# Three edits to a scheduled attention kernel: later loads, a values-stationary first layer, and another choice of the tiles whose exp runs on VectorE

## Chip, cores and metric

The kernel runs on one core of one Trainium2 chip. The metric is the device time of one execution in microseconds (us). A quoted time is the median of the runs of one kernel. All runs told of here are fast runs: none is over 1.5% above the fastest of the same kernel. A ratio is the mean time of one kernel's fast runs over the mean time of the kernel before in the same rounds on the same chip, so it is not quite the ratio of the medians quoted beside it. Intervals are 95%.

## The reference

Four layers act on 2048 tokens of width 512, with 32 heads of 16. Each is a layer norm, an attention, an output projection and a residual. Layers 0 and 2 are "memory attention", layers 1 and 3 full attention.

```python
# layers 0 and 2: four segments of 512 tokens
for s in range(4):
    p = softmax(qs @ ks.T / 4 + causal_mask)
    a_mem = phi(qs) @ M / (phi(qs) @ z + 1e-6)       # read-out of the memory
    outs.append(g * a_mem + (1 - g) * (p @ vs))      # g = sigmoid(beta), per head
    M = M + phi(ks).T @ vs;  z = z + sum(phi(ks))    # memory chain: s needs s-1
# layers 1 and 3: all 2048 keys
p = softmax(q @ k.T / 4);  o = p @ v
# every layer: x = x + attention(layernorm(x)) @ wo
```

A *block* (L, s) below is layer L with the queries of tokens 512·s to 512·s+511.

## The kernel before

A list scheduler, written in Python, runs while the kernel is built. It keeps an estimated clock for each engine and lays down one fixed, in-order program for TensorE (PE), ScalarE (ACT), VectorE (DVE), GpSimd (POOL) and the DMA queue.

The main loop goes: three score tiles (128×512 each) by PE into PSUM, one exp over all three by ScalarE into a ring of 18 buffers, then the products with V (PV) by PE. Projections, layer norms, memory work and evictions run as background threads between the groups.

```python
def emit_group(self, tiles, mode):             # scores -> exp, cut
    sc.add("pe", ... matmul(out, lhsT, rhs) ...)          # S, four row groups
    self.dx_scores(tiles, mode)                            # maybe one tile for VectorE
    sc.add("act", ... activation(dst, src, ACT.Exp, scale=SCALE) ...)   # 128x1536
    # masks on POOL for the diagonal blocks of layers 0 and 2
```

Some tiles leave ScalarE. A *dx group* is four score tiles whose exp is computed by VectorE: four evictions `dz` and seven arithmetic steps on 2048 columns. The rule that picks them before looks at the unit in work and asks for ten groups' worth of its tiles still unscored:

```python
def dx_pick(self):
    ...
    for u in seen:                              # the unit in work, and the next
        if u["kind"] != "B" or u["pvn"] < 12 or u["no"] < self.dx_no: continue
        rest = [tl for tl in u["tiles"] if not tl.get("dx") and "slot" not in tl]
        if len(rest) < 4 * (DX_LEFT + 1): continue         # DX_LEFT = 9
        four = rest[-4:]
def dx_scores(self, tiles, mode):
    if mode != "w" or len(tiles) < 3: return   # not in blocks with background work ("m")
def g_dx(self, four):                          # a thread; each yield lets others in
    o = dv(... tensor_scalar(F, lo, ...)); yield W(o)      # dF
    o = dv(... tensor_scalar(E, hi, ...)); yield W(o)      # dE
    ...                                                    # dP1 dP2 dP3 dP4
    o = dv(... tensor_tensor(E, E, Pz, ALU.add))           # dE2
```

In layers 0 and 2 the exp tile is stationary and V (17 columns per head: 16 and a one, for the sum) streams. The result is token-major, so a DMA transpose must turn it for the output projection, and its buffer `tokk` is the one that the memory chain uses for phi(k):

```python
def norm_A(self, u, par, bank, alloc):          # cut
    if s > 0: self.ensure(("nd", L, s))         # the memory read-out must be done
    dv(... reciprocal(r1, acc[:, :, 16]) ...)   # 128x16
    dv(... tensor_tensor(r2, r2, om, ALU.mult) ...)     # times 1-g
    dv(... tensor_tensor(dst, acc4, rb, ALU.mult) ...)  # into ot; adds a_mem if s > 0
    if self.cnt[key] == 8:
        zs = self.take_oT(L, s)
        if self.tok_mem is not None: self.ensure(("dM",) + self.tok_mem)
        for i in range(4): o = self.dma_T(self.tokk[...], self.ot[:, i, :], ...)
        self.set_ev(("otfree", L, s))
def t_mem(self, L, s, prio):                    # phi(k).T V, cut
        if self.oT_hold[0] is not None: yield ("ev", [("op",) + self.oT_hold[0]])
        for c in range(NCH): o = self.dma_T(self.tokk[...], self.kA[:, u, c, :], ...)
def t_nd(self, L, s, prio):                     # read-out phi(q) M into ot
        yield ("ev", [("M", L, s), ("otfree", L, s - 1)] + [("q", L, s, c) for c in range(NCH)])
# pv_ready: the last PV step of either half of a unit waits for ("nd", L, s)
```

All loads are issued at the start, ahead of the first transposes on the same queue:

```python
ld_x(0); ld_w(0, "A_wq"); ld_w(1, "A_wk"); ld_w(2, "A_wv")
for s in range(1, 4): ld_x(s)
# then beta, woA, wB (1.5 MB), woB
def g_ln(self, L, s):                           # cut
    for i, t in enumerate(t4):
        xn = self.xn[:, i % 2, :]               # two buffers
        o = sc.add("dve", ... tensor_scalar(xn, xt, mu, r1, ...))
        o = self.dma_T(self.xT[...], xn, ...)
```

The softmax here doesn't subtract the row's maximum and nothing guards it: scores larger than these inputs give would overflow.

## Time and profile before

The median of the first three runs is 2208.72 us (2208.08 to 2210.48). The profiled span is 2208.9 us.

The first line is that of the page of the kernel before for engine totals: busy time, share of the span, number of instructions.

```profile
PE 1735.5 (79%) x13064; PEld 458.4 (21%) x13138; DVE 1551.6 (70%) x2436; ACT 2011.4 (91%) x1594; POOL 263.4 (12%) x562
```

ScalarE, at 91%, looks like the limit, but the share is an average. The next lines are the table by stretch of the kernel before: start:end, length, then the busy time of each engine with its instruction count, the granted PE clock, the DMA share and GB/s.

```profile
0.00:75.00 75.00, 34.28 (x258) 12.45 (x262) 36.40 (x93) 25.90 (x31) 21.99 (x49) 0.86 0.45 120
75.00:370.00 295.00, 243.00 (x2396) 96.31 (x2418) 174.76 (x431) 235.22 (x224) 96.89 (x239) 0.76 0.10 19
370.00:500.00 130.00, 102.39 (x612) 18.57 (x609) 61.05 (x89) 129.46 (x104) 0.00 (x0) 0.52 0.00 1
500.00:1340.00 840.00, 662.92 (x5154) 184.04 (x5185) 642.01 (x983) 776.84 (x590) 116.96 (x206) 0.63 0.05 9
1340.00:1500.00 160.00, 132.71 (x1073) 41.02 (x1080) 55.11 (x130) 150.15 (x135) 27.60 (x69) 0.69 0.04 8
1500.00:2209.00 709.00, 560.23 (x3581) 106.02 (x3586) 582.30 (x716) 693.79 (x515) 0.00 (x0) 0.55 0.01 4
```

Read the fourth figure after the length, ACT. In the first two rows it is busy 25.9 + 235.2 of 370 us: 109 us are lost there. From 370 to 500 us it is full while VectorE works 61 of 130 us: there is room on VectorE for more of ScalarE's work. From 1500 us on ScalarE is saturated.

The start of the kernel before, in the timeline: start, length, engine, line, operation, names, shapes and count; in brackets the idle time before it and what ended it.

```profile
12.50 21.27 SPq L369 DMA_TRANSPOSE xT<-xn  x5
21.97 0.82 DVE L577 TENSOR_SCALAR xn<-x_tok,lnmv,lnr 128x512 bf16<-128x512 bf16 x2 [11.42 <-DMA xT<-xn]
26.27 3.57 PE L527 MATMUL ps<-xT,wA 128*128 128x512 bf16 x8 [23.83 <-DMA xT<-xn]
32.33 1.51 ACT L908 ACTIVATE pT<-ps 128x512 bf16<-128x512 f32 x2 [30.26 <-PE ps L902]
```

The third normalize waits 11.42 us for the buffer that the first transpose reads, the first projection starts at 26.27 us, and the first exp at 32.33 us. (The 21.27 us of the first line span five transposes and the pauses between them.)

Two groups of instructions of the kernel before matter later: columns as in the timeline without the times, then busy us, mean ns of one, and the idle time of the engine before them with its main releasers. The first is the exp (all shapes), the second the PV matmuls of layers 0 and 2.

```profile
L908 ACT ACTIVATE pT<-ps 128x1536 bf16<-128x1536 f32 (+1 forms) x1518 | 1977.7, 1463 | 159.3 <-PE ps L902 144.6 <-issue 3.5 <-PE ps L1018 3.1
L1112 PE MATMUL ps<-vA,pT 128*128 128x17 bf16 x2560 | 96.0, 175 | 16.3 <-POOL pT L931 7.6 <-DVE dz L1021 3.3 <-DVE q L542 1.8
```

Nearly all of ScalarE's idle time before an exp is ended by a score matmul: PE is late, for whatever reason. The 2560 narrow matmuls cost 96 us of PE time in both memory layers together; 43.9 us of it fall in layer 0.

### The profile page before, as it was taken

To read this page: it belongs to the slowest core of one execution; us is meant where nothing else is said; L and a number is where in the kernel's file an instruction comes from. 1 tells how busy PE (TensorE), PEld (TensorE's weight loads), DVE (VectorE), ACT (ScalarE), POOL (GpSimd) and SP (SyncE) were. 2 spreads that over 40 slices of the span, in tenths; PEclk is the share of its full clock that TensorE was granted. 3 is DMA by queue.
4 is the path that set the end of the run, shared out by engine and by line. 5 is a ranking of instruction groups with operands and counts; after the bars stand their busy time and mean duration, and the time that the engine had idled before them with its cause. 6 is when DMAs were issued, how large, how long until landed. Compare 5 with 4: busy or idle time off the path is not lost.

```text
span 2208.9 us, 32937 instructions
## 1 busy us (share of the span) xinstructions
PE 1735.5 (79%) x13064; PEld 458.4 (21%) x13138; DVE 1551.6 (70%) x2436; ACT 2011.4 (91%) x1594; POOL 263.4 (12%) x562
## 2 busy tenths in 40 slices
PE   3878887787778787777777888787778887787777
PEld 1333332111222112121122223221111111111111
DVE  4677534177888777887768766136778888888887
ACT  2778788998999979989989998999999999999998
POOL 2443230000023001220011201110000000000000
PEclk8778767556755775556856588566565555556555
DMA  5110100000000000000100000000000000000000
GB/s 143 30 30 11 20 11 20 0 1 13 8 1 1 20 18 2 1 10 11 20 1 1 11 11 11 1 20 1 1 10 1 1 10 1 1 1 11 1 1 10
DMA packets 73162, 26.25 MB, mean 12 GB/s; under 512 B 65840, under 2 KB 72496, under 8 KB 73008
## 3 DMA queue, kind: packets, MB, share of 16 engines
q1 hardware_dynamic: 73008, 24.14, 4.9%
q8 instruction: 103, 1.69, 0.3%
q14 instruction: 51, 0.42, 0.1%
HBM read 6.30 MB, written 2.10 MB: 4 GB/s over the span
## 4 chain that ended last, share of the span: by engine, by line
ACT 44%; PE 27%; issue 12%; DVE 11%; DMA 3%; POOL 2%; SPq 1%; ACTq 0%; DVEq 0%
ACT pT L908 43%; PE ps L527 10%; PE ps L902 9%; PE ps L1127 5%; DMA xT<-xn 2%; POOL pT L931 2%; PE ps L1112 2%; DVE dz L1021 1%; PE ps L1018 1%; DVE db L1063 1%; DVE dz L1061 1%; SPq L369 1%; DVE df L1046 1%; DVE lnst L559 1%; DMA tokk<-ot 1%
## 5 line engine op out<-in xcount | busy, mean ns | idle before, releaser
L908 ACT ACTIVATE pT<-ps 128x1536 bf16<-128x1536 f32 (+1 forms) x1518 | 1977.7, 1463 | 159.3 <-PE ps L902 144.6
L902 PE MATMUL ps<-q,kB 32*128 32x512 bf16 x3708 | 717.5, 554 | 289.5 <-ACT pT L908 283.3
L1127 PE MATMUL ps<-pT,vB 128*17 128x512 bf16 x3708 | 510.7, 547 | 12.5 <-DVE dz L1021 3.4
L1021 DVE TENSOR_SCALAR dz<-ps 128x512 int32<-128x512 f32 x388 | 267.3, 689 | 152.8 <-PE ps L1018 144.3
L931 POOL TENSOR_SCALAR_AFFINE_SELECT pT<-pT 128x256 bf16<-128x256 bf16 (+2 forms) x519 | 237.0, 486 | 721.0 <-ACT pT L908 719.6
L902 PEld LDWEIGHTS ps<-q,kB 32*128 32x128 bf16 x3708 | 132.6, 97 | 855.5 <-ACT pT L908 793.3
L1018 PE MATMUL ps<-q,kB 32*128 32x512 bf16 x388 | 227.1, 585 | 1.2 <-DVE dz L1021 1.1
L902 PE MATMUL ps<-q,kA 32*128 32x512 bf16 (+3 forms) x1024 | 134.5, 404 | 52.8 <-ACT pT L908 50.0
L1127 PEld LDWEIGHTS ps<-pT,vB 128*17 128x17 bf16 x3708 | 89.1, 90 | 375.6 <-issue 337.8
L1196 DVE STREAM_TRANSPOSE T<-ps 128x512 f32<-128x512 f32 x88 | 62.8, 713 | 130.0 <-PE ps L1127 128.5
L1046 DVE TENSOR_SCALAR df<-dz 128x2048 f16<-128x2048 uint16 x97 | 120.2, 1239 | 3.3
L1061 DVE TENSOR_TENSOR dz<-dz,df 128x2048 f16<-128x2048 f16 x97 | 119.6, 1233 | 2.7
L1057 DVE TENSOR_TENSOR dz<-dz,df 128x2048 f16<-128x2048 f16 x97 | 119.3, 1230 | 2.1
L1063 DVE TENSOR_TENSOR db<-db,dz 128x2048 int16<-128x2048 int16 x97 | 118.8, 1225 | 2.4
L1052 DVE TENSOR_SCALAR db<-dz 128x2048 int16<-128x2048 int16 x97 | 119.2, 1229 | 0.0
L1112 PE MATMUL ps<-vA,pT 128*128 128x17 bf16 x2560 | 96.0, 175 | 16.3 <-POOL pT L931 7.6
L527 PE MATMUL ps<-xT,wA 128*128 128x512 bf16 x239 | 74.2, 440 | 36.0 <-DMA xT<-xn 23.8
L1112 PEld LDWEIGHTS ps<-vA,pT 128*128 128x128 bf16 x2560 | 81.5, 102 | 76.2 <-POOL pT L931 51.2
L527 PE MATMUL ps<-xT,wB 128*128 128x512 bf16 x225 | 74.6, 459 | 14.4 <-DMA xT<-xn 6.9
L826 DVE TENSOR_TENSOR x_tok<-x_tok,ps 128x512 bf16<-128x512 bf16 x64 | 43.9, 687 | 57.1 <-PE ps L527 56.4
L577 DVE TENSOR_SCALAR xn<-x_tok,lnmv,lnr 128x512 bf16<-128x512 bf16 x64 | 25.9, 425 | 66.6 <-DMA xT<-xn 59.9
L1127 PE MATMUL ps<-db,vB 128*17 128x512 bf16 x388 | 56.6, 574 | 16.7 <-DVE db L1063 15.4
(79 smaller groups left out, 1071.3 us busy)
## 6 DMA issues: line engine op xcount, KB each, us to landing
x_tok<-in_A_x_dram SPq DMA_DIRECT2D x16, 128.0 KB, 4.5
out_dram<-x_tok SPq DMA_DIRECT2D x4, 512.0 KB, 2.9
wB<-in_B_wqkv_dram SPq DMA_DIRECT2D x1, 1536.0 KB, 8.4
xT<-xn SPq DMA_TRANSPOSE x64, 2.4
wA<-in_A_wq_dram SPq DMA_DIRECT2D x1, 512.0 KB, 4.3
wA<-in_A_wk_dram SPq DMA_DIRECT2D x1, 512.0 KB, 5.2
wA<-in_A_wv_dram SPq DMA_DIRECT2D x1, 512.0 KB, 6.4
woA<-in_A_wo_dram SPq DMA_DIRECT2D x1, 512.0 KB, 4.9
```

The costliest lines, as they stand in the source:

```text
L527: return self.sc.add("pe", lambda e: e.matmul(out, lhsT, rhs, start=start, stop=stop), reads=reads, bank_ops=[(bank, "w", alloc)], emit=la ...
L902: sc.add("pe", (lambda out, lhsT, rhs: lambda e: e.matmul(out, lhsT, rhs, start=True, stop=True))(out, lhsT, rhs), reads=reads, bank_ops=[ ...
L908: o = sc.add("act", lambda e: e.activation(dst, src, ACT.Exp, scale=float(SCALE)), writes=[self.b_pT[s0 + i] for i in range(n)], bank_ops= ...
L931: om = sc.add("pool", (lambda ap, pat: lambda e: e.affine_select(ap, ap, pattern=pat, compare_op=ALU.is_ge, fill=0.0, base=0, channel_mult ...
L1018: sc.add("pe", lambda e: e.matmul(out, lhsT, rhs, start=True, stop=True), reads=reads, bank_ops=[(bank, "w", alloc)], emit=True, name="SX" ...
L1021: o = sc.add("dve", lambda e: e.tensor_scalar(dst, out, float(EXP_C * 65536.0), -126.0 * 65536.0, op0=ALU.mult, op1=ALU.max), writes=[self ...
L1046: o = dv(lambda e: e.tensor_scalar(F, lo, 2.0 ** -16, -0.5, op0=ALU.mult, op1=ALU.add), bz, bF, "dF", 1.24)
L1057: o = dv(lambda e: e.tensor_tensor(Pz, Pz, F, ALU.mult), bF + bP, bP, "dP2", 1.24)
L1061: o = dv(lambda e: e.tensor_tensor(Pz, Pz, F, ALU.mult), bF + bP, bP, "dP4", 1.24)
L1063: o = dv(lambda e: e.tensor_tensor(E, E, Pz, ALU.add), bP + bE, bE, "dE2", 1.24)
L1112: sc.add("pe", (lambda o0, slot, p0, v, first: lambda e: e.matmul(self.ps[:, o0:o0 + 17], self.pT[:, slot, p0:p0 + 128], v, start=first, s ...
L1127: sc.add("pe", (lambda out, v, rhs, start, stop: lambda e: e.matmul(out, v, rhs, start=start, stop=stop, skip_group_check=True))(out, v, r ...
```

## The change

The intent has three parts.

**Loads.** Only the first segment and the three weights of layer 0 are loaded ahead. The rest is issued by a thread behind the transposes of each segment. The first segment's normalize uses four buffers.

**Layer 0 attention.** V becomes stationary, as in layers 1 and 3, and the exp tile streams. The result is normalized through 32×32 block transposes on VectorE, into its own buffers. The memory read-out is transposed by DMA into `m0` and added. The memory chain of layer 0 no longer shares a buffer with the output.

**VectorE exp.** The tiles of a dx group are picked by their distance: at least 56 tiles ahead, in any block from the end of layer 0 on. A group that will be needed soon goes ahead of other work on VectorE.

```diff
+DX_SLACK = 4.0
+DX_LEAD = 56
-DX_LEFT = 9
@@ setup
         ld_x(0)
+        ld_w(1, "A_wk")
         ld_w(0, "A_wq")
-        ld_w(1, "A_wk")
         ld_w(2, "A_wv")
-        for s in range(1, 4):
-            ld_x(s)
-        ... beta, woA, wB, woB at once
+        def rest():
+            yield ("ev", [("xT", 0, 0)])
+            ld_x(1)
+            ... beta, woA
+            yield ("ev", [("xT", 0, 1)])
+            ld_x(2)
+            ... wB in four chunks
+            yield ("ev", [("xT", 0, 2)])
+            ld_x(3)
+            ... woB
+        self.spawn(rest(), -1.0, "LD")
@@ g_ln
+            if L == 0 and s == 0 and i >= 2:
+                xn, bxn = self.ot[:, i, :], self.b_ot[i]
@@ t_nd
-            yield ("ev", [("M", L, s), ("otfree", L, s - 1)] + [("q", L, s, c) for c in range(NCH)])
+            yield ("ev", [("M", L, s)] + ([("otfree", L, s - 1)] if L > 0 else []) + [("q", L, s, c) for c in range(NCH)])
+            if L == 0:
+                yield ("ev", [("pvdone", L, s - 1)])
+                for i in range(4):
+                    self.dma_T(self.m0[:, :, i * 128:(i + 1) * 128], self.ot[:, i, :], ...)
@@ t_out
-            self.oT_hold[slot] = None
+            if L:
+                self.oT_hold[slot] = None
@@ unit_A: layer 0 with V stationary
+                    pv = [(None, par, j, 0, 512, 0, va(par, j, 0), vr(0))]
+                    ...
@@ norm, layer 0
+            dv(lambda e: e.scalar_tensor_tensor(on, T1[:, :, 0:16], om, rb, op0=ALU.mult, op1=ALU.mult), ...)
+                o = dv(lambda e: e.transpose(dst, onf), ...)
+                if s > 0:
+                    self.ensure(("nd", L, s))
+                    o = dv(lambda e: e.tensor_tensor(dst, dst, mem, ALU.add), ...)
@@ pv_ready
-        if last and u["kind"] == "A" and u["s"] > 0 and ("nd", ...) not in self.ev:
+        if last and u["kind"] == "A" and u["s"] > 0 and (u["L"] > 0 or u["pvd"] == 4) and ("nd", ...) not in self.ev:
@@ dx_pick
-            if len(rest) < 4 * (DX_LEFT + 1):
-                continue
+            n += far.get(id(u), len(rest))
+            if u["kind"] != "B" or u["no"] < self.dx_no or n < DX_LEAD or len(rest) < 8:
+                continue
@@ new
+    def dx_ahead(self, u, need):
+        ...                                   # n: tiles still to come before this group's PV
+        return DVE_AHEAD if 0.45 * n < need + DX_SLACK else DX_AHEAD
@@ dx_scores
-        if mode != "w" or len(tiles) < 3:
+        if ("op", 0, 3) not in self.ev or len(tiles) < 2:
             return
```

## The prediction

> **What bounds the kernel now.** The page shows ScalarE busy 91% of 2208.9 us; the chain that ended last puts 43% on the exp activation. The table by stretch splits this. From 1500 us to the end ScalarE is busy 693.8 of 709 us: saturated. From 370 to 500 us it is busy 129.5 of 130 while VectorE works only 61. From 500 to 1340 us: 777 of 840. In the first 370 us (layer 0 and the start of layer 1) only 261: 109 us are lost to latency, 31 of them before the first exp (32.3 us).
>
> **Startup.** All 6.3 MB of loads are issued by 12.5 us and the first four transposes come after them on the same queue. The first releases its buffer only at 21.97 us, while the median transpose takes 2.4 us. [...] The last of the four lands near 26.1. With only 1.5 MB of wA ahead, and four buffers, so that no normalize waits for a transpose, I expect it near 15: 10 to 12 us gained, all on the critical path.
>
> **Layer 0 attention.** 1280 matmuls of 17 columns (28 to 35 ns each) become 512 wide ones with V stationary, four side by side [...]. About 2560 columns a unit, at 0.55 us per four of 512, is 1.5 to 2.7 us against 2.2 to 2.8: an estimate, small gain. VectorE pays: a norm goes from 0.9 us (1.4 with memory) to transpose 0.71 + reciprocal 0.25 + scale 0.43, plus half of (0.71 + memory add about 0.4): some 20 us more over 32 norms. In return the output no longer shares the token-major buffer with phi(k), so the memory chain runs ahead, attention waits for it only before the last step of a unit, and output projection needs no DMA transposes. Of the 60 us of ScalarE idle between 75 and 370 us I expect 10 to 20 back. Evacuation copies on ScalarE rise by 22 (0.6 us each), which fills idle time and relieves VectorE by 15.
>
> **VectorE exp.** The built order has 107 groups instead of 97: 40 tiles leave ScalarE. In the saturated stretch ScalarE starts a group of three every 1.38 us, so a tile is worth about 0.45 us: 18 us at most. By unit: six more groups go to layer 1's first query block, nine to layer 3's first, five leave later blocks, where time is given back. VectorE pays 10.3 us a group, mostly where it idles. I expect 10 to 16 us net. PE waits on late VectorE groups (60 us in the list of waits) should shrink, but few of them reach ScalarE.
>
> **Sum.** 2208.7 - 11 - 4 (gates stall near 50 us) - 14 - 13 = about 2167 us (range 2142 to 2192). Chances: faster by over 2%: 0.45; within 2%: 0.52; slower: 0.03.
>
> **What would show it.** First exp near 20 to 22 us; ScalarE idle in the first 370 us falls from 109 to about 80; exp instructions 1501 instead of 1518; VectorE busy near 1660 us; the last stretch (layer 3, blocks 1 to 3) no shorter.
>
> **What would make it wrong.** Spread-out loads could delay later transposes of layer 0; the heavier VectorE norm could hold PSUM banks and stall PE; VectorE groups put first could delay evacuations, so that ScalarE idles more. On the good side, if the memory chain held layer 0, the gain there could be twice mine.

## The result

The changed kernel takes 2174.34 us (2173.01 to 2175.28, four runs) against 2209.6 us: ratio 0.984, interval 0.9823 to 0.9857. That is 35 us where 42 were predicted, inside the range and within 2%. A second measurement of the same kernel on another occasion (e9 below) gave 0.9837.

The totals of the changed kernel on its page:

```profile
PE 1706.2 (79%) x12290; PEld 426.3 (20%) x12370; DVE 1658.1 (76%) x2532; ACT 2004.1 (92%) x1599; POOL 274.9 (13%) x562
```

VectorE works 107 us more, as predicted (1660), ScalarE 7 us less. The table by stretch of the changed kernel, columns as before, without the last row:

```profile
0.00:75.00 75.00, 43.66 (x255) 13.88 (x260) 37.64 (x94) 40.34 (x47) 28.13 (x66) 0.82 0.46 118
75.00:370.00 295.00, 247.57 (x1786) 72.31 (x1806) 221.40 (x460) 261.28 (x256) 94.83 (x221) 0.78 0.09 17
370.00:500.00 130.00, 105.27 (x656) 19.46 (x654) 108.34 (x148) 127.84 (x98) 2.14 (x2) 0.54 0.02 5
500.00:1340.00 840.00, 652.93 (x5210) 185.01 (x5246) 633.24 (x979) 780.30 (x601) 116.99 (x206) 0.66 0.04 9
1340.00:1500.00 160.00, 125.38 (x1037) 36.61 (x1043) 122.56 (x210) 142.22 (x118) 32.84 (x69) 0.63 0.04 8
```

In the first 370 us ScalarE is now busy 40.3 + 261.3 us, so 68 us idle instead of 109: the gain is there. (At fixed times the two tables hold different work. Within layer 0 alone ScalarE was idle 97.6 of 327.0 us and is idle 59.5 of 296.8.) Look then at the last row: VectorE has gone from 55 to 123 us of work, as intended, yet ScalarE does not finish its own reduced work at the old pace. It was idle 9.9 us in this stretch and is now idle 17.8; over the whole of block (3,0) it is idle 10.4 of 275.1 us before and 21.4 of 270.1 now.

The start of the changed kernel in the timeline:

```profile
10.52 2.60 SPq L377 DMA_TRANSPOSE xT<-xn  x2
13.16 2.58 SPq L377 DMA_TRANSPOSE xT<-ot  x2
17.10 3.57 PE L553 MATMUL ps<-xT,wA 128*128 128x512 bf16 x8 [14.66 <-DMA xT<-ot]
19.62 0.69 DVE L585 BATCH_NORM_STATS2 lnst<-x_tok 128x6 f32<-128x512 bf16 x1 [8.16 <-DMA x_tok<-in_A_x_dram]
23.29 0.32 DVE L642 TENSOR_SCALAR q<-q,parm 128x512 bf16<-128x512 bf16 x1
24.16 0.60 ACT L960 ACTIVATE pT<-ps 128x512 bf16<-128x512 f32 x1 [1.72 <-PE ps L954]
```

The first projection starts 9.2 us earlier, the first exp 8.2 us earlier (24.16 against 32.33). The four transposes hold the queue for 5.2 us (10.52 to 15.74). Between projection and exp, VectorE first waits for the second segment's data, 8.16 us, and computes its statistics; the scaling of q that the first scores need stands behind that in VectorE's order.

The exp group of the changed kernel, and the PV matmuls of layer 0, which are now four widths of one line:

```profile
L960 ACT ACTIVATE pT<-ps 128x1536 bf16<-128x1536 f32 (+1 forms) x1501 | 1962.1, 1471 | 123.6 <-PE ps L954 92.4 <-PE ps L1086 14.4 <-issue 14.2
L1201 PE MATMUL ps<-pT,vA 128*17 128x512 bf16 x128 | 15.4, 457 | 7.2 <-POOL pT L983 3.4 <-DVE T L1273 2.3 <-DVE kA L568 1.3
L1201 PE MATMUL ps<-pT,vA 128*17 128x384 bf16 x128 | 13.8, 382 | 0.3 <-POOL pT L983 0.2
L1201 PE MATMUL ps<-pT,vA 128*17 128x256 bf16 x128 | 11.4, 321 | 0.1
L1201 PE MATMUL ps<-pT,vA 128*17 128x128 bf16 x128 | 8.7, 249 | 0.0
```

Two things to see. The idle time before exps fell from 159 to 124 us, but 14.4 us of it is now ended by L1086, the score matmul of a dx group, which hardly appeared before (3.1 us), and 14.2 us is "issue" (3.5 before). And the 512 wide matmuls of layer 0 sum to 49.3 us, but matmuls of different widths overlap: counted once, they keep PE busy 38.5 us. The narrow ones of layer 0 did so for 43.9 us, with 1240 of 1280 in the trace, and for 45.4 us in the trace of e1 below, which has all. So the swap saved some 7 us of PE time.

### Where the time went, block by block

The build knows which exp instruction belongs to which block, so the k-th exp of the trace gives the end of each block. Worked out in this way from the traces of the kernel before, of the changed kernel, and of e4 below (loads and attention, old dx choice), in us:

| stretch (by last exp) | before | e4: no new dx | changed | dx groups, old → new |
|---|---|---|---|---|
| start to end of (0,3) | 327.0 | 298.1 | 296.8 | 0 |
| (1,0) | 186.6 | 188.0 | 177.1 | 4 → 10 |
| (1,1) | 252.3 | 252.8 | 261.5 | 15 → 13 |
| (1,2) | 273.3 | 266.6 | 262.5 | 14 → 14 |
| (1,3) | 274.4 | 272.9 | 274.2 | 13 → 12 |
| (3,0) | 275.1 | 273.7 | 270.1 | 4 → 13 |
| (3,1) to (3,3) | 610.1 | 612.3 | 617.0 | 47 → 45 |
| after the last exp | 10.1 | 10.1 | 12.8 | |

A memory layer's blocks lie inside those of its neighbours; layer 2's projections, memory read-outs and attention run within (1,1) to (3,0). Of the 36.9 us between the spans of the two traces, 30.2 come by the end of layer 0. Between e4 and the changed kernel, the new dx choice gains 10.9 us in (1,0), where it was said to, but only 3.6 us in (3,0), where nine groups were added; (1,1) and the last blocks give back 13.4. Small differences between blocks are not to be read: the trace of e9 below, the same program again, has 619.5 us for (3,1) to (3,3), and e12, whose order on every engine is the same up to 1344 us, has 174.0 us for (1,0).

The four largest gaps on ScalarE lie in (1,2), (1,3) and (3,0), as the timeline of ScalarE in the changed kernel shows (gaps in brackets):

```profile
832.93 4.13 ACT L960 ACTIVATE pT<-ps 128x1536 bf16<-128x1536 f32 x3 [5.71 <-issue]
842.96 101.07 ACT L960 ACTIVATE pT<-ps 128x1536 bf16<-128x1536 f32 x75 [5.90 <-PE ps L954]
1098.21 4.13 ACT L960 ACTIVATE pT<-ps 128x1536 bf16<-128x1536 f32 x3 [7.30 <-issue]
1358.31 6.92 ACT L960 ACTIVATE pT<-ps 128x1536 bf16<-128x1536 f32 x6 [9.20 <-PE ps L1086]
```

What happens in the longest is seen on all engines of the changed kernel just before 1358 us:

```profile
1349.77 0.41 PE L553 MATMUL ps<-Mr,ph 128*128 128x136 bf16 x2 [1.24 <-DVE ot L791]
1350.46 1.22 DVE L1124 TENSOR_SCALAR db<-dz 128x2048 int16<-128x2048 int16 x1
1352.56 0.41 PE L553 MATMUL ps<-Mr,ph 128*128 128x136 bf16 x2 [1.55 <-DVE ot L791]
1353.25 0.68 DVE L1127 TENSOR_SCALAR dz<-df 128x2048 f16<-128x2048 f16 x1
1356.57 1.22 DVE L1129 TENSOR_TENSOR dz<-dz,df 128x2048 f16<-128x2048 f16 x1
1356.80 0.79 PE L1184 MATMUL ps<-vA,pT 128*128 128x17 bf16 x24 [1.52 <-DVE q L568]
```

PE runs the memory read-out of layer 2's last segment (`Mr,ph`), a short matmul pair at a time. Each pair waits until VectorE has evicted an earlier one (L791). Between those evictions VectorE puts steps of a dx group (L1124, 1.22 us, and L1127, 0.68 us); a third (L1129, 1.22 us) comes after them, before the scaling of q. The scores stand behind the read-out in PE's order, so they wait, and ScalarE with them.

### The profile page after: what moved, and what is told of

Read it like the earlier page. It is cut to its first block, busy times and chain, and to the rows that moved or that the text cites. A ratio compares the mean times of both kernels' runs of the same rounds, so it can differ in the third digit from the quotient of the medians.

```text
span 2172.0 us, 31457 instructions
## 1 busy us (share of the span) xinstructions
PE 1706.2 (79%) x12290; PEld 426.3 (20%) x12370; DVE 1658.1 (76%) x2532; ACT 2004.1 (92%) x1599; POOL 274.9 (13%) x562
## 4 chain that ended last, share of the span: by engine, by line
ACT 47%; PE 25%; issue 14%; DVE 9%; POOL 2%; DMA 2%; SPq 1%; ACTq 0%; DVEq 0%; POOLq 0%
ACT pT L960 46%; PE ps L954 9%; PE ps L553 8%; PE ps L1201 6%; POOL pT L983 2%; PE ps L1086 1%; DMA xT<-xn 1%; SPq L377 1%; DVE dz L1089 1%; PE ps L1184 1%; DVE T L1273 1%; DMA x_tok<-in_A_x_dram 1%; DVE lnst L585 1%; DVE df L1118 1%; DVE db L1124 0%
## 5 line engine op out<-in xcount | busy, mean ns | idle before, releaser
L1201 PE MATMUL ps<-pT,vB 128*17 128x512 bf16 x3668 | 498.4, 541 | 7.9 <-DVE x_tok L860 2.2
L1089 DVE TENSOR_SCALAR dz<-ps 128x512 int32<-128x512 f32 x428 | 294.8, 689 | 193.5 <-PE ps L1086 182.3
L1086 PE MATMUL ps<-q,kB 32*128 32x512 bf16 x428 | 246.1, 576 | 1.2 <-DVE dz L1089 1.0
L1118 DVE TENSOR_SCALAR df<-dz 128x2048 f16<-128x2048 uint16 x107 | 131.9, 1233 | 3.6
L1135 DVE TENSOR_TENSOR db<-db,dz 128x2048 int16<-128x2048 int16 x107 | 131.3, 1227 | 2.9
L1133 DVE TENSOR_TENSOR dz<-dz,df 128x2048 f16<-128x2048 f16 x107 | 131.2, 1226 | 2.8
L1129 DVE TENSOR_TENSOR dz<-dz,df 128x2048 f16<-128x2048 f16 x107 | 131.1, 1225 | 2.2
L1124 DVE TENSOR_SCALAR db<-dz 128x2048 int16<-128x2048 int16 x107 | 131.3, 1227 | 1.9 <-PE ps L1201 1.9
L1273 DVE STREAM_TRANSPOSE T<-ps 128x512 f32<-128x512 f32 x120 | 85.1, 709 | 37.3 <-PE ps L1201 36.4
L553 PE MATMUL ps<-xT,wA 128*128 128x512 bf16 x237 | 74.4, 446 | 21.1 <-DMA xT<-ot 14.7
L860 DVE TENSOR_TENSOR x_tok<-x_tok,ps 128x512 bf16<-128x512 bf16 x64 | 43.8, 686 | 46.1 <-PE ps L553 45.7
L1127 DVE TENSOR_SCALAR dz<-df 128x2048 f16<-128x2048 f16 x107 | 74.2, 693 | 0.5
L1131 DVE TENSOR_SCALAR dz<-dz 128x2048 f16<-128x2048 f16 x107 | 73.7, 689 | 1.0
```

Of the source, the lines that this page charges most:

```text
L553: return self.sc.add("pe", lambda e: e.matmul(out, lhsT, rhs, start=start, stop=stop), reads=reads, bank_ops=[(bank, "w", alloc)], emit=la ...
L1086: sc.add("pe", lambda e: e.matmul(out, lhsT, rhs, start=True, stop=True), reads=reads, bank_ops=[(bank, "w", alloc)], emit=True, name="SX" ...
L1089: o = sc.add("dve", lambda e: e.tensor_scalar(dst, out, float(EXP_C * 65536.0), -126.0 * 65536.0, op0=ALU.mult, op1=ALU.max), writes=[self ...
L1118: o = dv(lambda e: e.tensor_scalar(F, lo, 2.0 ** -16, -0.5, op0=ALU.mult, op1=ALU.add), bz, bF, "dF", 1.24)
L1124: o = dv(lambda e: e.tensor_scalar(E, hi, 128.0, 16256.0 + 53.0, op0=ALU.mult, op1=ALU.add), bz, bE, "dE", 1.24)
L1129: o = dv(lambda e: e.tensor_tensor(Pz, Pz, F, ALU.mult), bF + bP, bP, "dP2", 1.24)
```

## Experiments

There are twelve kernels in three calls of four; the kernels of one call ran on one chip and share the runs of the kernel before. The build with all three parts switched off or on gives exactly the instructions of the kernel before or of the changed kernel.

| run | what it is | median us | ratio to before | interval |
|---|---|---|---|---|
| e1 | loads alone | 2199.37 | 0.9939 | 0.9926–0.9953 |
| e2 | layer 0 attention alone | 2185.66 | 0.9893 | 0.9875–0.9911 |
| e3 | dx choice alone | 2211.44 | 0.9994 | 0.9981–1.0006 |
| e4 | loads and attention, old dx choice | 2176.61 | 0.9835 | 0.9822–0.9849 |
| e5 | changed, memory chain of layer 0 tied back | 2185.29 | 0.9884 | 0.9869–0.9898 |
| e6 | changed, new dx choice in (1,0) only | 2207.67 | 0.9985 | 0.9972–0.9998 |
| e7 | changed, dx held during memory read-outs of layer 2 | 2168.36 | 0.9808 | 0.9792–0.9825 |
| e8 | changed, second segment loaded ahead | 2191.03 | 0.9911 | 0.9897–0.9925 |
| e9 | changed, again | 2176.44 | 0.9837 | 0.9824–0.9851 |
| e10 | changed, dx steps cut to 8 columns (wrong result) | 2145.06 | 0.9702 | 0.9689–0.9715 |
| e11 | e4, dx steps cut to 8 columns (wrong result) | 2164.70 | 0.9796 | 0.9782–0.9809 |
| e12 | changed, dx held in the last read-out only | 2167.58 | 0.9802 | 0.9784–0.9819 |

The median of the kernel before is 2212.65, 2212.41 and 2210.77 us in the three calls; a ratio becomes us below by multiplying by these.

### e1_load_only, e2_attention_only, e3_dx_only, e4_no_dx: the parts

Edit: each of the three parts of the diff above is applied alone (e1 to e3), or the first two together (e4).

```diff
 e1: before.py + the hunks of setup (rest) and g_ln
 e2: before.py + the hunks of unit_A, norm, t_mem, t_nd, t_out, pv_ready
 e3: before.py + the hunks of dx_pick, dx_ahead, dx_scores, run
 e4: e1 + e2
```

> Only the load order and the two extra normalize buffers are changed; attention of layer 0 and the choice of VectorE exp are as before. Theory A (the three parts add up, each worth what the comparison of the two traces by block says): the first exp starts near 24 us instead of 32.3, and these 8 us are kept to the end: about 2201 us. Rival B (layer 0 is held by its own chain of memory and output projection, so that an earlier start is mostly absorbed by that chain): under 4 us faster, about 2206, with the end of the last layer 0 exp no earlier than 324 us instead of 327.

Measured: 0.9939, 13.5 us gained. In its trace the first exp is at 24.1 us, and the last exp of layer 0 is 10.3 us earlier than before; the gain is kept to the end. What the loads gain at the start is gained in the whole; it is not absorbed by layer 0's own chain, which rival B had, nor taken back by loads that delay later transposes, a risk that the prediction named. e1 changes the order of the loads and the two extra buffers together, and they were not separated. In the trace before, the first transpose lands 9.4 us after its issue, behind the loads; the third is issued at 22.41 us, after its normalize has waited for the first one's buffer.

> Only layer 0 attention is changed (values stationary, block transposed norm, own output buffers, memory chain free of them); loads and VectorE exp as before. Theory A: ScalarE idle inside layer 0 falls, the last layer 0 exp ends about 22 us earlier (305 instead of 327), and the program takes about 2187 us. Rival B (parts need each other: the chain can only run ahead when the inputs come earlier): under 12 us faster, above 2197.

Measured: 0.9893, 23.7 us. Its five runs fall into two clusters, near 2185 and near 2194 us; the two slower ones show granted clocks of 0.635 and 0.631, the others 0.639 and 0.640. The trace is of one of the faster. In it, 14.4 us are gained by the end of layer 0 (theory A had 22), 3.2 us in (1,0), which is no more than (1,0) differs between runs of one order, and 6.7 us in (1,2). That last block has the same number of matmuls (1595) and of VectorE instructions (328) as before, but the granted clock there is 0.62 against 0.58. So a quarter of this part's gain comes from a place that it does not touch. e4 shows the same there, and so does e3, which leaves layer 0 as it was (264.4 us at 0.62). Why the clock is higher there has not been tested.

> Only the choice of tiles for the VectorE exp is changed: 107 groups instead of 97, 13 exp instructions fewer on ScalarE or more. Theory A: layer 1's first query block is about 10 us shorter, and of the rest nothing is gained: layer 3's first block loses 38 tiles but gains only 5 us, and later blocks with fewer groups give it back; total 5 to 9 us faster, about 2202. Rival C (the 18 us that the 40 tiles are worth are there, and what ate them in the changed kernel was a collision with the other two parts): 14 to 18 us faster, about 2193.

Measured: 0.9994; the interval holds "no gain", and both theories missed. In its trace (1,0) to (3,0) take 1246.0 us against 1261.7, but (3,1) to (3,3) take 620.4 against 610.1.

> The changed kernel with the old choice of tiles for the VectorE exp (97 groups). Theory A: about 30 us faster than before (2179), 5 to 8 us slower than the changed kernel. If the new choice is worth its full 18 us in the whole, it is only 18 us faster than before (2191). If it is worth nothing, it equals the changed kernel at 2174.

Measured: 0.9835, 36.5 us, equal to the whole change (0.984 and, in e9, 0.9837). The loads' 13.5 and the attention's 23.7 sum to 37.2, so the two add up. The dx choice adds nothing; theory A's 5 to 8 us for it were missed.

### e5_chain_tied: is the freed memory chain what pays in layer 0?

```diff
-            yield ("ev", [("M", L, s)] + ([("otfree", L, s - 1)] if L > 0 else []) + ...)
+            yield ("ev", [("M", L, s)] + [("otfree", L, s - 1)] + ...)
-            if L:
-                self.oT_hold[slot] = None
+            self.oT_hold[slot] = None
             if self.cnt[k3] == 4:
+                if A:
+                    self.take_oT(L, s)
+                    if self.tok_mem is not None:
+                        self.ensure(("dM",) + self.tok_mem)
-        if last and ... and (u["L"] > 0 or u["pvd"] == 4) and ("nd", u["L"], u["s"]) not in self.ev:
+        if last and ... and ("nd", u["L"], u["s"]) not in self.ev:
```

> The changed kernel (2174) with layer 0's memory chain tied back to the output as it was before: the phi(k) transposes wait for the output projection of the segment before, the memory read-out waits for the segment's output, and both halves of a unit wait for the read-out; values stay stationary, with the new norm. Theory A1 (the 24 us of the attention part come from the freed chain): 15 us or more slower than the changed kernel, 2189 or more. Rival A2 (they come from the new PV matmuls, the norm and the missing transposes of the output): within 6 us of the changed kernel, below 2180.

Measured: 0.9884, 25.7 us, so 10 us of the gain are lost. That lies between what A1 and A2 expected; as numbers both missed. The trace says where: layer 0 ends at 309.6 us instead of 296.8, 12.8 us later, of which some 3 are made up later. By the same measure, attention gains 18.6 us in layer 0 when loads are already changed (316.7 in e1, 298.1 in e4). So the freed chain is the larger part of the attention's gain in layer 0, about two thirds, and the rest, with wide matmuls, evictions and other order, has not been split further.

### e6_dx_early_block: the new choice only where it gained

```diff
-            if u["kind"] != "B" or u["no"] < self.dx_no or n < DX_LEAD or len(rest) < 8:
+            if u["kind"] != "B" or u["L"] != 1 or u["part"] is None or u["no"] < self.dx_no or n < DX_LEAD or len(rest) < 8:
+            if four is None and mode == "w" and len(tiles) == 3:
+                four = self.dx_pick_old()      # the rule of before, for all other units
+        # the priority (DVE_AHEAD) only for units of (1,0) as well
```

> The changed kernel with the new choice of VectorE tiles in layer 1's first query block alone (10 groups there as in the change), the old choice from then on; 105 groups. The run without the new choice took 2176.6. Theory D1 (the new choice is worth 12 us in layer 1's first block, and is given back later): about 2165, the first block ends near 474 us as in the changed kernel, and the stretch from there to the end is as long as in the run without the new choice (1688 us) or a little shorter. Rival D2 (a gain in that block is always given back, since the rest has less VectorE time or other work has been moved into it): 2174 or more.

Measured: 2207.67 us, 0.9985: far above what D1 expected, and so far above the bound of D2 that this is not the loss that D2 means either. The gain of (1,0) was there: the block ends at 472.8 us, (1,1) at 731.5. Then (1,2) to (3,0) take 852 us where the changed kernel takes 807. The timeline of e6 shows the worst of the gaps:

```profile
1260.00 1.22 DVE L1155 TENSOR_SCALAR db<-dz 128x2048 int16<-128x2048 int16 x1
1268.38 1.89 PE L554 MATMUL ps<-xT,wB 128*128 128x512 bf16 x4 [3.96 <-DVE q L569]
1276.76 1.22 DVE L1166 TENSOR_TENSOR db<-db,dz 128x2048 int16<-128x2048 int16 x1
1278.72 0.53 PE L1232 MATMUL ps<-db,vB 128*17 128x512 bf16 x4
1280.45 1.45 ACT L961 ACTIVATE pT<-ps 128x1536 bf16<-128x1536 f32 x1 [18.60 <-PE ps L955]
```

A dx group is in progress from L1155 to L1166, 17 us for steps that sum to some 7, because evictions of projections go ahead of it. Its PV (L1232) stands in PE's order at 1278.72 us, and ScalarE is empty for 18.6 us. So here a dx group without the priority, placed elsewhere by a change in an earlier block, did harm; that the missing priority is the cause was not tested, and e4, whose groups have none either, shows no gap above 7.71 us after layer 0. This run answers another question than was asked: the order is fragile, and here the gain in one block was not kept by undoing the rule in the others.

### e7_hold_dx_in_readout and e12_hold_last_readout: take the collision away

```diff
 def t_nd(...):
+            self.nd_busy = L > 0               # e7;  e12: L > 0 and s == 3
             for i in range(4): ...             # the read-out loop
+            self.nd_busy = False
 def dx_scores(...):
-        if ("op", 0, 3) not in self.ev or len(tiles) < 2:
+        if ("op", 0, 3) not in self.ev or len(tiles) < 2 or self.nd_busy:
 def run(self):
-                if k == "pe":
+                if k == "pe" or k == "dx" and self.nd_busy:
                     continue
```

> The changed kernel with VectorE exp work held back while layer 2's memory read-out runs (eight pairs of matmuls with three VectorE steps each). Theory D3 (what layer 3's first block loses is the ScalarE stall of 9.2 us at 1349 us, where exp steps stand between the read-out's steps on VectorE): the stall there falls below 4 us, the block is about 7 us shorter, the whole 2164 to 2170. Rival D4 (the stall is the read-out's own; exp steps in it hardly matter, the held steps come back as a wait elsewhere): 2172 to 2178.

Measured: 0.9808, about 6 us better than the changed kernel, which ran in other calls (0.984 and 0.9837). In (3,0) ScalarE's idle time fell from 21.4 to 14.7 us and the gap in the last read-out from 9.20 to 5.6 us, so the collision (D3) was a real part of it, though the gap did not fall below 4 us as D3 had it. The hold also moved one dx group from (3,0) to (3,1). In the other two read-outs the hold made new gaps, of 14.2 us (at 838 us) and 12.8 us (at 1104 us); what made these was not followed up.

That pointed to holding in the last read-out alone.

> The changed kernel with VectorE exp held back only during the memory read-out of layer 2's last segment, since holding it in all of them shortened layer 3's first block by 4.6 us and the one behind it by 2.8, but lengthened the two blocks before (+3.4, +1.4). Theory D3: 7 us faster than the changed kernel on the same chip, 3 us faster than holding in all: ratio to before about 0.980. Rival D4 (what the hold gains comes back as waits): within 3 us of the changed kernel.

Measured: 2167.58 us, 0.9802 against 0.9837 of the changed kernel in the same rounds, with intervals that just do not overlap: 8 us faster than the changed kernel, 43.8 us faster than before, with a correct result. ScalarE's timeline of e12 at the same place:

```profile
1352.15 6.92 ACT L963 ACTIVATE pT<-ps 128x1536 bf16<-128x1536 f32 x6 [5.61 <-PE ps L957]
```

The gap is 5.61 us, and it is ended by an ordinary score matmul. (3,0) takes 266.4 us instead of 270.1, with one dx group fewer, and (3,1) to (3,3) 614.4 instead of 617.0, with one more; so not all of the 8 us is the end of the collision. (1,0) is shorter too (174.0 against 177.1), but that is not the edit's doing: up to 1344 us every engine has the order of the changed kernel. From (3,0) on, e12 is 7 us shorter than the changed kernel's trace and 9 us shorter than that of e9. It is the best correct version run, level with e7 within the noise.

### e8_x1_early: the statistics of the second segment ahead of q

```diff
         ld_w(2, "A_wv")
+        bt = self.new_batch("x1")
+        sc.add_dma("sp", lambda e: e.dma_start(self.x_tok[:, 4:8, :], xv[:, 4:8, :]), bt, writes=self.b_x[4:8], name="dx1")
+        self.set_ev(("x", 0, 1))
 def rest():
-            ld_x(1)
```

> The changed kernel with the second segment's input loaded by one DMA behind the first weights, ahead of the first transposes. The trace of the changed kernel shows VectorE waiting 8.2 us for that load, and then doing its statistics (19.6 to 23.3 us) ahead of the first query scaling, which the first exp waits for. Theory S1: first exp at about 22 us instead of 24.2, layer 0's first segment 3 to 6 us shorter, total 4 to 6 us faster, about 2169. Rival S2 (transposes wait again behind the extra load, and the segment is bound otherwise): first exp at 24 us or later and no gain.

Measured: 0.9911, 16 us slower than the changed kernel, and both theories missed. The statistics did move, to 11.7–15 us, but the first exp came at 24.0 us, as before the edit: q's scaling (23.18 us) now stands on VectorE behind three evictions of projections (19.16 to 23.26 us), which ScalarE did in the changed kernel. Layer 0 ends 3.3 us later. The rest of the loss is far from the edit: (1,1) to (3,0) take 1090 us instead of 1068. The scheduler placed dx groups differently ((1,2) 11 instead of 14, (1,3) 15 instead of 12, (3,0) 10 instead of 13) and gaps of 9.8, 15.1 and 11.0 us appear on ScalarE at 979, 1118 and 1378 us.

### e9_changed_again, e10_changed_hollow_dx, e11_old_choice_hollow_dx: are the missing microseconds VectorE's?

The seven arithmetic steps of each dx group are cut from 2048 to 8 columns (except `dE`, which stays whole so that every buffer is written). The result is wrong (relative errors 0.024 and 0.023). The order of instructions on all engines is exactly that of the uncut kernel; only their length on VectorE is cut. What is left of a group is mostly its four evictions and `dE`: VectorE's busy time falls by 5.2 us a group (1658.1 to 1101.5 us), about half of it. GpSimd's falls with it, from 274.4 to 238.6 us, as its masks became faster too: 246.1 us in e9, 212.8 us in e10, a mean of 503 against 437 ns.

```diff
-        lo = bcast_ap(zf.bitcast(dt.uint16)[:, 0:1], [[2, 2048]])
+        lo = bcast_ap(zf.bitcast(dt.uint16)[:, 0:1], [[2, 8]])
-        F = self.df[:, :, :].rearrange("p a b -> p (a b)")
+        F = self.df[:, :, :].rearrange("p a b -> p (a b)")[:, 0:8]
         # Pz likewise, and E in the last step
```

> The changed kernel once more, to have it on the same chip and in the same rounds as the runs beside it: ratio to before 0.982 to 0.986, as at first. Every theory expects this.

> The changed kernel with six of the seven steps of each VectorE exp group cut to 8 columns (the dE step stays whole); results are wrong on purpose. The order of instructions on every engine is the same as in the changed kernel; only VectorE time falls, by some 6 us a group, about 640 us in all. Theory D5 (the 18 us that the new choice takes off ScalarE are eaten by waits for VectorE, either for a late exp group or for evacuations and read-out steps standing behind exp steps): the ScalarE stalls of 5.7, 5.9, 7.3 and 9.2 us near 832, 842, 1098 and 1358 us shrink below 3 us each, the kernel is 20 to 35 us faster, and it is then 12 to 20 us faster than the same cut made in the run without the new choice. Rival D6 (a tile off ScalarE is simply worth less than 0.45 us, since TensorE or the spacing of groups bounds the stretch; or the stalls are the read-out's own): under 10 us faster, and within 5 us of the cut run without the new choice.

> The same cut in the kernel with the new loads and layer 0 attention but the old choice of tiles (97 groups; 2176.6 uncut). Theory D5: 10 to 20 us faster than uncut, and 12 to 20 us slower than the changed kernel with the same cut. Rival D6: within 5 us of the changed kernel with the same cut.

Measured: 0.9837, 0.9702 and 0.9796. The old choice gains 9 us from a VectorE exp cut by half (0.9835 in e4 to 0.9796; D5 had 10 to 20), the new choice 30 us. With the cut the new choice is 19.6 us faster than the old (2145.06 against 2164.70); with VectorE's full time it is worth nothing. By stretch, from the traces:

| stretch | old → new choice, VectorE at full length (e4 → changed) | old → new choice, steps cut (e11 → e10) | estimate: tiles moved × 0.45 us |
|---|---|---|---|
| (1,0) | −10.9 | −11.1 | −10.8 |
| (1,1) | +8.7 | +4.0 | +3.6 |
| (1,2) | −4.1 | −9.4 | 0 |
| (1,3) | +1.3 | +2.0 | +1.8 |
| (3,0) | −3.6 | −10.1 | −16.2 |
| (3,1) to (3,3) | +4.7 | +2.6 | +3.6 |
| sum of these | −3.9 | −22.0 | −18.0 |

The estimate takes four tiles per group from the table above, with the 0.45 us a tile of the prediction. The sum with the steps cut, −22.0, is near the estimate, but in part by luck: −9.4 of it lies in (1,2), where no tile moved. There the two kernels differ in the granted clock (the figure before the last two); the rows of (1,2) in e10 and in e11:

```profile
723.70:981.50 257.80, 201.19 (x1585) 52.38 (x1595) 134.27 (x316) 244.44 (x187) 28.65 (x68) 0.63 0.04 9
732.40:999.60 267.20, 210.87 (x1595) 53.27 (x1602) 137.53 (x327) 246.65 (x189) 29.73 (x68) 0.59 0.05 9
```

Without (1,2) the sums are +0.2 with full steps and −12.6 with steps cut, against −18.0. So most of the gain of 40 tiles exists, and the length of VectorE's steps eats it, above all in (1,1) and (3,0); a share of GpSimd's faster masks in this was not separated. In the whole, the 19.6 us are what D5 expected and far from D6's 5. But D5 also had each of the four gaps shrink below 3 us. ScalarE's timeline of e10 (all its times are earlier) shows the gaps that are left:

```profile
825.72 101.03 ACT L960 ACTIVATE pT<-ps 128x1536 bf16<-128x1536 f32 x75 [5.90 <-PE ps L954]
1076.82 4.13 ACT L960 ACTIVATE pT<-ps 128x1536 bf16<-128x1536 f32 x3 [2.17 <-issue]
1331.64 9.20 ACT L960 ACTIVATE pT<-ps 128x1536 bf16<-128x1536 f32 x8 [8.21 <-PE ps L1086]
```

The gap of 5.71 us is gone and that of 7.30 fell to 2.17, but 5.90 is as it was and 9.20 only fell to 8.21: two of four, so here D5 missed. The large gaps are only part of it. The exp group of e10 gives the total:

```profile
L960 ACT ACTIVATE pT<-ps 128x1536 bf16<-128x1536 f32 (+1 forms) x1501 | 1960.7, 1507 | 93.0 <-PE ps L954 75.2 <-PE ps L1086 10.4 <-issue 3.6
```

Idle time before exps is 93.0 us, against 127.0 us in e9, the uncut kernel: 34 us less, which is the whole difference of the two spans (35.3 us). In e10 the gap in (3,0) is about as long as with full steps, because the one long step between the evictions there is `dE`, which was not cut. The timeline of e10:

```profile
1324.32 1.22 DVE L1124 TENSOR_SCALAR db<-dz 128x2048 int16<-128x2048 int16 x1
1326.43 0.41 PE L553 MATMUL ps<-Mr,ph 128*128 128x136 bf16 x2 [1.55 <-DVE ot L791]
```

PE waits 1.55 us behind it, as in the changed kernel. So e10 does not speak against the collision; e12, which takes `dE` out of the read-out too, shortened the gap to 5.61 us, and that rest is there without any dx step. How a wait for VectorE reaches ScalarE in each place (through the PSUM banks, the 18 buffers, or the PV that stands in PE's order) is argued from timelines only. A longer ring was not tried.

## Why the prediction was right or wrong

**The time: right, 2174 in 2142 to 2192, with the class "within 2%" as the likelier one.** Two terms were too small and one was far too large, and they nearly cancelled, so that the sum came so close is in part luck.

**Startup (−11): right.** e1 measures 13.5 us. The mechanism is as told: with all loads issued ahead of it, the first transpose landed 9.4 us after its issue, against a median of 2.4 us over all 64; with the loads moved, the first ones land after 2.4 to 2.5 us, and the first projection starts at 17.10 instead of 26.27 us. The first exp at 24.2 us missed the stated 20 to 22: the four transposes hold the queue 5.2 us, about 1.3 us each, one behind the other, so they land near 17 and not 15, and q's scaling stands behind another segment's statistics. e8 shows that the latter is not cured by an earlier load alone.

**Layer 0 attention and gates (−14 and −4): right in kind, a little small.** e2 measures 23.7 us, e4 minus e1 23.0. By the end of layer 0 its trace gains 14.4 us (18.6 with the loads in place), which is the predicted size. The rest comes mostly in (1,2), outside the layer, which the prediction did not foresee. The stall that the prediction calls "gates" (computing g and 1 − g on VectorE near 50 us) was not measured by itself, but the traces show where it went: ScalarE's gap there, 8.7 us before (until 56.1 us), is still 8.2 us in e2, but 3.0 us in e1 and 2.9 in the changed kernel. So it is the loads that shortened it, not the new attention (in e1 alone another gap, of 7.7 us until 65.7 us, comes instead). The wide matmuls saved some 7 us of PE time (45.4 to 38.5 us), the prediction's "small gain"; the freed memory chain is the larger part of the gain in layer 0 (e5), which the prediction named as its good side.

**VectorE exp (−13): wrong.** Measured about 0 (e3 0.9994; e4 0.9835 against 0.9837 and 0.984). The counts were right: 107 groups, 1501 exps, VectorE busy 1658 us. The rate of 0.45 us a tile was about right where VectorE had room: (1,0) gave −10.9 us for 24 tiles, an estimated −10.8. With VectorE's steps cut, the stretches where tiles moved gave −12.6 of an estimated −18.0. The step that failed is "VectorE pays 10.3 us a group, mostly where it idles". VectorE idles in (3,0) on average (135 of 274 us busy in e4), but not at the moment: in the last read-out a step put between two evictions kept PE waiting for 1.55 us, whatever the average. In (3,0), 36 tiles should have brought 16 us and brought 3.6. PE's waits for late VectorE groups (the prediction's 60 us) did not shrink either: 66 us in the changed kernel. The sentence about "VectorE groups put first" that delay evictions "so that ScalarE idles more", listed as a risk, is what the last read-out shows; e12, which takes away the collision there alone and moves one group on, gets 8 us.

**"The last stretch no shorter": right.** (3,1) to (3,3) take 617.0 us against 610.1, 4.7 us of it against e4, where 3.6 are the two groups fewer. Another 2.7 us are lost after the last exp. The chain of waits ends with the last output projection. Before:

```profile
2201.73 2.99 PE ps L527 x13
```

In the changed kernel:

```profile
2162.15 5.74 PE ps L553 x13
```

The same 13 matmuls took 5.74 us against 2.99 us; the clock granted while they ran was 0.50 against 1.00 (0.61 from 2157 us to the end against 0.78 from 2197 us), and the two durations, a factor of 1.9, agree with that. What sets the clock at the end was not tested. It is not the order alone: e1 and e4 with the old choice take 2.98 us for these 13 matmuls (granted clock 0.76 over the last 13 us of both), e7 and e8 with the new choice 5.2 and 5.3 (0.61 over the last 15 us of both), but e9, which has exactly the order of the changed kernel, takes 4.33, its last matmuls coming every 0.22 us instead of 0.43.

**Left open:** the split of what is not the freed chain in layer 0, the higher clock in (1,2) (0.62 against 0.58), the clock of 0.54 in (3,1) to (3,3), where PE is busy 485.7 of 610.1 us in the kernel before, the clock at the end, and the placement of dx groups that would bring the 13 to 20 us that e10 and e11 show to be there.

## What to carry to other kernels

An idle share of an engine is no room by itself: before giving it work, look at what else it does in that stretch and who waits for it in order; here two steps of 1.22 and 0.68 us between short evictions, on which PE's next matmuls hung, were a part of a gap of 9.20 us that fell to 5.61 without them. To learn whether a missing gain was lost to an engine's time or never existed, cut that engine's work with the order unchanged, and compare both choices (e10, e11); but check what the cut leaves standing (`dE` here) and look at stretches that the choice does not touch ((1,2) here). In a kernel whose order is made by a scheduler, a local edit is not local: e6 and e8 lost about 33 and 16 us against the changed kernel, mostly far from the edit, so test parts by their end-to-end time as well as by their blocks.
